# A fused attention and mixer kernel: a pair's keys loaded whole and first, and an order made with other times to landing

## The chip, the cores and the metric

The kernel runs on one core of one Trainium2 chip. The metric is the device time of one execution in microseconds (us). A core has five engines with a queue of instructions each: TensorE (PE; its weight loads are listed as PEld), VectorE (DVE), ScalarE (ACT), GpSimd (POOL) and SyncE (SP), which here issues every DMA.

## The reference

Three blocks follow one another, all in float32, with batch 4, 448 tokens and 768 channels:

- Attention, 12 heads of 64: `q` and `k` are divided by their root mean square along the head and multiplied by `g_q` and `g_k`; `scores = q_n k_n^T / 8`; softmax over the keys; times `v`.
- A gated mixer: `h = relu(x w_in)` (1024 wide), halves `u` and `v`; `v` is normalised, mixed over the tokens by `w_spatial` (448 x 448) plus a bias; `(u * v_s) w_out`.
- A second mixer: over the tokens (448 to 256 to 448) with a residual, then over the channels (768 to 1536 to 768) with a residual.

The softmax sums over all keys of a head, so the keys may stand in any order as long as the values stand in the same one.

## The kernel before, in words

Attention handles two heads at a time, a pair; there are 24 pairs (four batches of six). `Attention.load` (L593) fetches a pair's `q` and `k` into one tile `raw` of 112 partitions: 448 tokens are 4 chunks of 112, both heads side by side. There are two `raw` buffers. The 448 keys of a head are also cut as three chunks of 128 and a rest of 64 for the product with `v`; the rests of both heads are put together into one chunk of 128. For that the rest of the first head must stand at the end of its row of scores and the rest of the second at its beginning. In the kernel before the second head's keys are therefore loaded rotated, in three DMAs: the last 64 tokens first (64 rows), then the first 48 to fill the chunk, then the other 336. With two DMAs for `q` and one for the first head's `k` a pair takes six. `load_v` (L610) fetches `v` in four DMAs: for each head three chunks of 128, and the 64 of the rest into `vrest`.

`norms` (L622) squares and sums a pair on ACT and DVE (`sq`, `ss`; the half with `q` first, then the half with `k`; there is one `sq` buffer) and makes the factors `ra`, `ry`, `rz` on POOL and ACT; `scale` multiplies `raw` on POOL; `transposed` turns `q` and then `k` on PE into `tp` and copies it out (`whole` for the first eight pairs, `qt` and `kt` after them). `scores` (`sc`, `nm`, `e`), `normalise`, `turned` (`tp`, `et`) and `values` (`av`) follow. `start` (L751) does the first pair and loads the second; `slot` (L773) interleaves pair s with its neighbours and loads pair s + 2.

Beside attention run three kinds of work: conversions of weights on ACT, DVE and POOL (`word`, `wv`, `wpart`), of which the pieces of `prepare_uo` and `prepare_next` go through two buffers each of `wraw` and `wpart` and are stored to scratch in DRAM (`wu_d`, `wo_d` and others); and the first mixer, batch by batch (`vps`, `ups`, `sps`, `xps` on PE), which reads these weights back as `wu` and `wo`. After them come the token mixer (`h1ps`, `u_ps`) and the channel mixer (`h2ps`, `o_ps`).

The order in which every engine issues is not that of the source. All instructions are recorded in a `Plan`, each with a cost from `estimate` (L214): the time that it holds its engine and the lateness with which its result reaches the next engine. `issue` (L364) then places them by list scheduling on these costs: forward by priority, backward for new priorities, eight rounds, and the order of the shortest plan is issued, so that all instructions have the line L405 in the profile. For a DMA the costs are

```
        return max(475, shape[0] * n * 4 / 260), 2000
```

that is, SP is taken to be busy for 475 ns or for the bytes at 260 bytes a ns, and the data usable 2000 ns later. Every engine, SP too, issues strictly in the planned order.

Of the kernel before, what the change touches and what calls it, by code (L numbers as in the profile page):

```python
# [149 lines left out]
class Plan:  # L150
# [63 lines left out]
    def estimate(self, engine, fn, out, ins, kwargs):  # L214

        shape = max((tuple(x.shape) for x in [out] + ins if isinstance(x, Part)), key=free)
        n = free(shape)
        psum = any(x.tile.psum for x in ins)
        if engine == "tensor":
            if fn == "transpose":  # L220
                return ins[0].shape[0] / 1.2 + 3, 200
            n = free(ins[1].shape)
            if ins[1].dtype == F32R:
                return 0.326 * n if ins[0].shape[0] <= 64 else n / 2.4 + 13, 200
            if ins[0].shape[0] <= 64:
                return 1.04 * n, 200
            return n / 1.2 + 54 if out.shape[0] <= 64 else n / 0.6, 200
        if engine == "scalar":
            extra = any(isinstance(kwargs.get(k), Part) for k in ("bias", "scale"))
            extra += kwargs.get("accum_out") is not None  # L230
            return 0.833 * n + (51 if psum else 94) + 93 * extra, 142
        if engine == "vector":
            if n <= 64:
                return 160, 128
            if fn in ("tensor_scalar", "tensor_copy") and not psum:
                return 0.53 * n + 90, 128
            pointer = fn == "scalar_tensor_tensor" and any(free(x.shape) == 1 for x in ins)
            return 1.042 * n + 70 + 61 * pointer, 175 if free(out.shape) < n else 128
        if engine == "gpsimd":
            if fn == "tensor_scalar":  # L240
                return max(165, 1.3 * n + 35), 75
            pace = 2.0 if any(x.steps and x.steps[-1][0] == "to_broadcast" for x in ins) else 2.4
            return max(165, pace * n + 20), 75
        return max(475, shape[0] * n * 4 / 260), 2000

    def fence(self, pools, act):

# [173 lines left out]
def free(shape):  # L421
    n = 1
    for x in shape[1:]:
        n *= x
    return n
# [11 lines left out]
def attention_moe_mixer(  # L437
# [7 lines left out]
    nc = tc.nc  # L445
# [6 lines left out]
    P = 128  # L452
    C = 4
    T = S // C
# [10 lines left out]
    LAST, R = TOK[-1]  # L465
# [74 lines left out]
    nc = Plan(nc)  # L540
# [42 lines left out]
    class Attention:  # L583
# [9 lines left out]
        def load(self, i):  # L593
            if not 0 <= i < NP:
                return
            b, j = divmod(i, KD)
            t = self.p.tile([T, 2, C, 2, D], F32, tag="raw", bufs=2, name="raw")
            for r in range(2):
                nc.sync.dma_start(
                    out=t[:, 0, :, r], in_=q[b, 2 * j + r].rearrange("(c p) d -> p c d", p=T))  # L600
            nc.sync.dma_start(out=t[:, 1, :, 0], in_=k[b, 2 * j].rearrange("(c p) d -> p c d", p=T))

            src = k[b, 2 * j + 1]
            nc.sync.dma_start(out=t[:R, 1, 0, 1], in_=src[LAST:])
            nc.sync.dma_start(out=t[R:, 1, 0, 1], in_=src[:T - R])
            nc.sync.dma_start(
                out=t[:, 1, 1:, 1], in_=src[T - R:LAST].rearrange("(c p) d -> p c d", p=T))
            self.raw[i] = t

        def load_v(self, i):  # L610
            if not 0 <= i < NP:
                return
            b, j = divmod(i, KD)
            t = self.p.tile([P, 2, C - 1, D], F32, tag="v32", bufs=VB, name="v32")
            rest = self.rests[i % VB]
            for r in range(2):
                src = v[b, 2 * j + r]
                nc.sync.dma_start(out=t[:, r], in_=src[:LAST].rearrange("(c p) d -> p c d", p=P))
                nc.sync.dma_start(out=rest[r * R:(r + 1) * R, r], in_=src[LAST:])
            self.v32[i] = t, rest  # L620

        def norms(self, i):  # L622
# [597 lines left out]
    n = NP + 1  # L1220
# [84 lines left out]
```

## Time and profile before

| | |
|---|---|
| median of 3 runs | 956.19 us (954.49 to 959.67) |
| the profiled execution | 952.84 us, its span 951.1 us |
| PE busy | 915.1 us, 96% of the span |
| DVE busy | 567.9 us, 60% |
| ACT busy | 452.1 us, 48% |
| POOL busy | 370.1 us, 39% |
| DMA | 118.58 MB |

The span is the time from the first to the last recorded instruction; the execution's own time is 1.74 us longer. Matmuls are pipelined and their ends are modelled, so what counts of PE is where it has nothing to do rather than its busy share.

### The profile page before, as it was taken

To read this page: it belongs to the slowest core of one execution; us is meant where nothing else is said; L and a number is where in the kernel's file an instruction comes from. 1 tells how busy PE (TensorE), PEld (TensorE's weight loads), DVE (VectorE), ACT (ScalarE), POOL (GpSimd) and SP (SyncE) were. 2 spreads that over 40 slices of the span, in tenths; PEclk is the share of its full clock that TensorE was granted. 3 is DMA by queue.
4 is the path that set the end of the run, shared out by engine and by line. 5 is a ranking of instruction groups with operands and counts; after the bars stand their busy time and mean duration, and the time that the engine had idled before them with its cause. 6 is when DMAs were issued, how large, how long until landed. Compare 5 with 4: busy or idle time off the path is not lost.

```text
span 951.1 us, 15484 instructions
## 1 busy us (share of the span) xinstructions
PE 915.1 (96%) x5328; PEld 736.9 (77%) x5328; DVE 567.9 (60%) x1254; ACT 452.1 (48%) x1135; POOL 370.1 (39%) x538
## 2 busy tenths in 40 slices
PE   3898999999999999999999999999999999999998
PEld 1344366668767777677889999899898998999898
DVE  4787878775776767764151367534665556555434
ACT  5887877777676777765342345301312213122100
POOL 3767766785666664654124123101201102011100
PEclk9998999999999999999999999999999999999999
DMA  6544465666534565332673475721211212111024
GB/s 153 138 101 134 116 172 149 158 188 184 163 92 107 172 207 179 97 98 99 220 223 129 142 246 181 266 85 34 78 56 36 64 34 83 50 51 50 17 89 144
DMA packets 124654, 118.58 MB, mean 125 GB/s; under 512 B 74784, under 2 KB 108128, under 8 KB 123040
## 3 DMA queue, kind: packets, MB, share of 16 engines
q1 hardware_dynamic: 124576, 117.59, 41.0%
q8 instruction: 42, 0.69, 0.3%
q14 instruction: 36, 0.29, 0.1%
HBM read 89.77 MB, written 27.79 MB: 124 GB/s over the span
## 4 chain that ended last, share of the span: by engine, by line
PE 82%; ACT 5%; DVE 5%; DMA 3%; issue 2%; POOL 2%; SPq 1%; ACTq 0%; POOLq 0%; DVEq 0%
PE o_ps L405 18%; PE h2ps L405 18%; PE tp L405 9%; PE av L405 6%; PE xps L405 6%; PE ups L405 6%; PE sc L405 6%; PE sps L405 4%; PE u_ps L405 3%; PE h1ps L405 3%; PE vps L405 3%; ACT e L405 2%; DVE nm L405 1%; SPq L405 1%; DMA x<-x_d 1%
## 5 line engine op out<-in xcount | busy, mean ns | idle before, releaser
L405 PE MATMUL o_ps<-c,h 128*128 128x384 f32 x1008 | 179.7, 337 | 0.0
L405 PE MATMUL h2ps<-ut,c 128*128 128x512 f32 (+1 forms) x864 | 178.9, 364 | 0.0
L405 PEld LDWEIGHTS o_ps<-c,h 128*128 128x128 f32 x1008 | 175.0, 188 | 2.0 <-DVE acc L405 0.5
L405 PEld LDWEIGHTS h2ps<-ut,c 128*128 128x128 f32 x864 | 148.1, 189 | 24.3
L405 POOL TENSOR_SCALAR e<-e,sums 112x448 f32<-112x448 f32 x192 | 122.8, 656 | 63.0 <-DVE sums L405 35.1
L405 POOL TENSOR_TENSOR c<-word,c 128x384 fp32r<-128x384 f32 x40 | 40.5, 1014 | 265.1 <-ACT c L405 241.7
L405 ACT ACTIVATE e<-sc,nm 112x448 f32<-112x448 f32 x192 | 120.0, 637 | 29.1 <-PE tp L405 15.0
L405 DVE TENSOR_REDUCE nm<-sc 112x1 f32<-112x448 f32 x192 | 110.0, 614 | 22.3 <-PE sc L405 22.0
L405 PEld LDWEIGHTS tp<-ident,e 112*128 112x128 f32 x672 | 75.3, 142 | 47.0 <-POOL e L405 16.6
L405 PE MATMUL tp<-ident,e 112*128 112x112 f32 x672 | 101.9, 267 | 6.4 <-POOL e L405 3.2
L405 DVE TENSOR_TENSOR acc<-o_ps,acc 128x384 f32<-128x384 f32 x140 | 77.2, 555 | 29.6 <-PE o_ps L405 28.9
L405 ACT ACTIVATE h<-h2ps 128x512 fp32r<-128x512 f32 (+1 forms) x48 | 25.8, 538 | 116.5 <-PE h2ps L405 114.9
L405 ACT ACTIVATE c<-word 128x384 fp32r<-128x384 f32 x40 | 21.0, 525 | 123.0 <-DVE word L405 58.2
L405 DVE SCALAR_TENSOR_TENSOR h<-h2ps,h 128x512 fp32r<-128x512 f32 (+1 forms) x48 | 29.9, 624 | 82.3 <-ACT h L405 82.2
L405 ACT ACTIVATE et<-tp 128x448 f32<-128x448 f32 x120 | 63.4, 544 | 20.5 <-PE tp L405 19.9
L405 PE MATMUL ups<-xp,wu 128*128 128x448 f32 x288 | 69.6, 379 | 1.4 <-ACT vr L405 0.7
L405 PE MATMUL av<-et,v 128*64 128x448 f32 x288 | 67.4, 563 | 0.0
L405 PE MATMUL xps<-wo,g 128*128 128x256 f32 x432 | 63.3, 291 | 0.1
L405 PEld LDWEIGHTS xps<-wo,g 128*128 128x128 f32 x432 | 55.1, 190 | 5.0 <-issue 2.3
L405 PEld LDWEIGHTS ups<-xp,wu 128*128 128x128 f32 x288 | 51.7, 189 | 8.6 <-ACT vr L405 1.1
L405 DVE TENSOR_SCALAR word<-word 128x384 f32<-128x384 f32 (+1 forms) x92 | 34.2, 372 | 37.1 <-ACT word L405 35.7
L405 PE MATMUL vps<-wv,xp 128*128 128x512 f32 x216 | 55.1, 402 | 0.0
(105 smaller groups left out, 1414.5 us busy)
## 6 DMA issues: line engine op xcount, KB each, us to landing
raw<-in_moe_w_ch_dram SPq DMA_DIRECT2D x40, 384.0 KB, 3.2
wu<-wu_d SPq DMA_DIRECT2D x16, 768.0 KB, 5.1
wo<-wo_d SPq DMA_DIRECT2D x12, 1024.0 KB, 5.1
raw<-in_q_dram SPq DMA_DIRECT2D x48, 112.0 KB, 3.0
acc<-u_d SPq DMA_DIRECT2D x14, 384.0 KB, 8.2
out_dram<-o SPq DMA_DIRECT2D x28, 192.0 KB, 1.9
v<-in_v_dram SPq DMA_DIRECT2D x48, 96.0 KB, 2.6
x_d<-xo SPq DMA_DIRECT2D x36, 128.0 KB, 2.4
```

Of the source, the lines that this page charges most:

```text
L405: getattr(getattr(self.nc, op.engine), fn)(*args, **kwargs)
```

## The change

`load` fetches `k` of both heads in their natural order with one DMA each, and before `q`. A pair takes four DMAs instead of six. So that the rests still meet in one chunk, the second head's rest of keys is its first 64 tokens, and `load_v` fetches its values to match: the three chunks of 128 from token 64 on and the rest from the first 64. The lateness of a DMA in `estimate` becomes 2400 ns plus 1.2 ns for every 1000 bytes. What SP itself is taken to cost is the same formula as before. The whole order is planned anew on these numbers.

```diff
-        return max(475, shape[0] * n * 4 / 260), 2000
+        size = shape[0] * n * 4
+        return max(475, size / 260), 2400 + 1.2e-3 * size
...
-            for r in range(2):
-                nc.sync.dma_start(
-                    out=t[:, 0, :, r], in_=q[b, 2 * j + r].rearrange("(c p) d -> p c d", p=T))
-            nc.sync.dma_start(out=t[:, 1, :, 0], in_=k[b, 2 * j].rearrange("(c p) d -> p c d", p=T))
-
-            src = k[b, 2 * j + 1]
-            nc.sync.dma_start(out=t[:R, 1, 0, 1], in_=src[LAST:])
-            nc.sync.dma_start(out=t[R:, 1, 0, 1], in_=src[:T - R])
-            nc.sync.dma_start(
-                out=t[:, 1, 1:, 1], in_=src[T - R:LAST].rearrange("(c p) d -> p c d", p=T))
+            for a, src in ((1, k), (0, q)):
+                for r in range(2):
+                    nc.sync.dma_start(
+                        out=t[:, a, :, r], in_=src[b, 2 * j + r].rearrange("(c p) d -> p c d", p=T))
             self.raw[i] = t
...
                 src = v[b, 2 * j + r]
-                nc.sync.dma_start(out=t[:, r], in_=src[:LAST].rearrange("(c p) d -> p c d", p=P))
-                nc.sync.dma_start(out=rest[r * R:(r + 1) * R, r], in_=src[LAST:])
+                tiles, others = (src[R:], src[:R]) if r else (src[:LAST], src[LAST:])
+                nc.sync.dma_start(out=t[:, r], in_=tiles.rearrange("(c p) d -> p c d", p=P))
+                nc.sync.dma_start(out=rest[r * R:(r + 1) * R, r], in_=others)
```

## Rows read from the trace of the kernel before

**Rows 1.** Stretches: start:end, length, each engine's busy us (instructions), granted clock, DMA.

```profile
0.00:20.00 20.00, 5.29 (x18) 2.72 (x20) 6.44 (x13) 8.48 (x17) 6.99 (x20) 1.00 0.64 159
20.00:120.00 100.00, 86.81 (x469) 40.08 (x470) 81.86 (x180) 84.44 (x232) 73.86 (x118) 0.97 0.46 123
120.00:180.00 60.00, 57.03 (x336) 37.26 (x335) 49.16 (x138) 45.35 (x127) 39.32 (x62) 1.00 0.58 162
180.00:460.00 280.00, 279.17 (x1803) 204.87 (x1802) 181.90 (x433) 192.61 (x521) 171.42 (x268) 1.00 0.49 146
```

**Rows 2.** Waits of PE over the whole span: us in total, times, longest.

```profile
PE tp L405 <- POOL raw L405: 12.9, 1, 12.9
PE sc L405 <- ACT e L405: 4.9, 6, 1.5
...
PE sc L405 <- ACT whole L405: 3.2, 2, 1.8
```

**Rows 3.** Timeline of SP, first 14 us: start, length, instruction, count.

```profile
0.74 0.92 SPq L405 DMA_DIRECT2D raw<-in_q_dram  x2
1.71 2.18 SPq L405 DMA_DIRECT2D raw<-in_k_dram  x4
3.93 0.48 SPq L405 DMA_DIRECT2D g<-in_g_q_dram  x1
...
5.73 0.59 SPq L405 DMA_DIRECT2D g<-in_g_k_dram  x1
...
7.53 2.13 SPq L405 DMA_DIRECT2D raw<-in_k_dram  x4
9.71 0.47 SPq L405 DMA_DIRECT2D raw<-in_moe_w_in_dram  x1
```

**Rows 4.** Timeline of the other engines at the start; in brackets idle time and releaser.

```profile
3.78 0.63 ACT L405 ACTIVATE sq<-raw 112x512 f32<-112x512 f32 x1 [1.76 <-DMA raw<-in_q_dram]
...
5.62 0.63 ACT L405 ACTIVATE sq<-raw 112x512 f32<-112x512 f32 x1 [1.22 <-DMA raw<-in_k_dram]
...
8.11 0.16 DVE L405 TENSOR_TENSOR gg<-g 128x1 f32<-128x1 f32 x1 [2.99 <-DMA g<-in_g_k_dram]
8.19 0.68 DVE L405 TENSOR_REDUCE ss<-sq 112x8 f32<-112x512 f32 x1
...
8.96 0.20 POOL L405 TENSOR_SCALAR ra<-ss 112x16 f32<-112x16 f32 x1 [7.37 <-DVE gg L405]
...
12.89 1.76 PE L405 MATMUL tp<-ident,raw 112*128 112x112 f32 x8 [12.89 <-POOL raw L405]
...
14.79 0.66 ACT L405 ACTIVATE word<-raw 128x512 f32<-128x512 f32 x1 [2.74 <-DMA raw<-in_moe_w_in_dram]
15.36 0.53 ACT L405 ACTIVATE whole<-tp 128x448 f32<-128x448 f32 x1
15.78 0.63 ACT L405 ACTIVATE whole<-tp,gg 128x448 f32<-128x448 f32 x1
...
16.46 4.71 PE L405 MATMUL sc<-whole 64*112 64x448 f32 x12 [1.81 <-ACT whole L405]
```

**Rows 5.** Waits of ACT on DMAs between 20 and 180 us.

```profile
ACT wpart L405 <- DMA wo_d<-wpart: 1.3, 1, 1.3
ACT wpart L405 <- DMA wu_d<-wpart: 0.9, 3, 0.4
```

**Rows 6.** Pieces of SP's queue in the chain of waits, 120 to 180 us.

```profile
132.20 0.34 SPq L405
...
173.20 0.45 SPq L405
```

**Rows 7.** The page's DMA issues: count, KB each, median us to landing.

```profile
raw<-in_q_dram SPq DMA_DIRECT2D x48, 112.0 KB, 3.0
```

**Rows 8.** Two stretches in which the granted clock fell.

```profile
70.00:76.00 6.00, 5.12 (x23) 3.27 (x24) 3.39 (x7) 4.04 (x10) 5.50 (x12) 0.72 0.31 97
84.00:90.00 6.00, 4.61 (x16) 1.60 (x16) 4.89 (x10) 4.21 (x14) 5.73 (x11) 0.72 0.50 178
```

**Rows 9.** Instructions of `ups`: ns min/median/max, first and last start.

```profile
L405 PE MATMUL ups<-xp,wu x288: 358/368/475, 157.5 to 511.9; 128*128 128x448 f32 x144
```

## The prediction

> **What bounds the kernel now.** I read the busy time by stage first. PE is the bound nearly everywhere: from 180 to 460 us it is idle for 0.83 of 280 us, so nothing that only makes a load earlier can gain there. It has room in three stretches [rows 1]: 14.7 us of the first 20, 13.2 of the 100 after them, 3.0 of the 60 up to 180. In the second of these no engine is full (PE 87, ACT 84, DVE 82 us of 100): work hands over from engine to engine there, and the order decides. Then PE's list of waits: one wait of 12.9 us for the first scaled `raw`, and 3.2 us for `whole` in two waits [rows 2]; most of both lies in the first 17 us. So I read that start instruction by instruction.
>
> There SP is what sets the pace. It issues without a pause from 0.74 us on, some 0.54 us an issue (four take 2.18) [rows 3]. Behind the sixteen issues of two pairs and the four small `g` the first load of `w_in` is issued at 9.71 and usable at 14.79. ACT stands still 2.74 us for it, because `word` is ahead of `whole` in ACT's order; the `tp` that `whole` reads began at 12.89. Both copies then end at 16.41 and the first scores start at 16.46 [rows 4].
>
> **The change part by part.** *Two issues fewer a pair, at the start.* Four issues fewer stand before `w_in`: 4 x 0.54 = 2.2 us, so it is issued at 7.55 and, with the same 5.08 us to use, `word` runs at 12.6 to 13.3. The chain of norms has to be as early, and there `k` first works against it: the first `sq` reads `q`, which now is issued last. The fourth issue starts at 0.74 + 0.46 + 0.51 + 0.54 = 2.25; before, `q` was usable 2.58 after its second issue began (1.20 to 3.78), so `sq` of `q` runs 4.83 to 5.46, about a microsecond later than now, its sum (0.68) to 6.2, `sq` of `k` to 6.85, since there is one buffer, and its sum to 7.6. The `g` loads are issued 1.08 earlier, so `gg` moves from 8.11 to 7.03; if the second sum stays behind it, it ends at 7.9. `ra` comes at 7.6 to 7.9 instead of 8.96, PE's `tp` at 11.5 to 11.9 and ends by 13.6 [rows 3, 4]. The second `whole` can start at 13.7 behind `word` and the first `whole`, and the scores at 14.4 instead of 16.46: 2.0 us. Bounds: 2.2, all that the issues take, and 0, if something else that the plan puts ahead on ACT takes the place. I take 2.0, the value nearest to the rows.
>
> What the Trainium skill's page "DMA: Bandwidth & Descriptors" (section "Issuing engines are not separate DMA queues") says speaks against this: the time that a sequencer takes to initiate a DMA is usually small relative to the DMA. By that rule fewer issues would be worth nothing, 956.2 us, the first rival below. At the start of this trace it does not hold: 8.9 us of issues stand in front of a load that lands in 5.08.
>
> *Does the gain reach the end?* After 180 us PE has no idle time to swallow it. Between 20 and 180 it could be swallowed by a later chain that starts on its own; `load`, `norms` and conversions all hang on the same start, so I keep it whole; the other end, 0, is the first rival.
>
> *Two issues fewer in the other 22 pairs.* 44 x 0.54 = 24 us of SP. SP mostly waits there and is not the bound: the only waits of ACT on DMAs from 20 to 180 are 2.2 us, for buffers that stores hold, none for `raw` [rows 5]. In the chain of waits SP's queue has seven pieces longer than 0.05 us from 120 to 180, 2.7 us together [rows 6]. The bounds are 0 and 2.7; the value taken is 0.5, as a raw load's issues are a part of these only. After 180 nothing.
>
> *`k` before `q`, the other 64 tokens as the rest.* The bytes, the four DMAs for `v` and all the arithmetic stay. The loads run a pair ahead and ACT never waits for `raw` after the start, so the order within a load is hidden by that lead: 0; if the lead is gone, the microsecond worked out above for each pair.
>
> *The new times to landing.* They are costs of the plan, not work. For 112 KB the plan's landing goes from 475 + 2000 to 475 + 2538 ns; the trace has 3.0 us [rows 7], so the new number is right there. What a better number can give back directly is a wait for a load that was believed too early, and those are the 2.2 us just named, and the start. What remains is that the whole order is drawn anew. The trace bounds this only roughly: at best the 16.2 us of idle from 20 to 180 go, and with them the two falls of the granted clock to half, 1.2 GHz, each after PE had waited for other engines; they cost 2 x 6 x 0.28 = 3.4 us [rows 1, 8]. At worst PE starves longer: 6 us, the slower rival. Nothing in the rows leans to a side; I take 0.
>
> **Sum.** 952.84 - 2.0 - 0.5 = 950.3 us against the profiled execution (span 951.1 and 1.74 around it). The three runs have their median at 956.19, 3.35 above that execution, and their lowest above it too; on their scale the forecast is 953.7 us, and 952 to 955.5 is its own range.
>
> **The rivals.**
> - *The start's gain is lost*, behind another instruction on ACT or in the mixed stretch up to 120 us, or because `q` as the last load holds the norms: 956.2. For it: the work of ACT and DVE there is 84 and 82% and does not shrink. Against: PE must do the same work and starts earlier.
> - *The new order closes gaps.* If a third of the 16.2 us of idle and of the 3.4 us of clock goes, 6.5 us, on top of the start: 956.2 - 2.0 - 6.5 = 947.7; 944 to 951. For it: no engine is full in that stretch, and these gaps are hand-overs that an order can hide. Against: almost none of them is a wait for a DMA, the one cost that was corrected.
> - *The new order starves PE: slower.* A weight piece of 256 KB holds one of two buffers for a load and then a store of 128 KB each way. In the new plan the load is later by 715 ns and the store by 557: 1.27 us a round, and 12 rounds of two for the 24 pieces of `wu` and `wo` make 15 us. If the plan gives way there, the first `ups`, now at 157.5 [rows 9], comes at about 173, and PE has nothing to fill its gaps with. Then the idle share of 20 to 120, 13.2%, lasts from 120 to 173 or to 205: 7.0 or 11.2 us in place of 3.0 [rows 1], less the 2.0 of the start: 958.2 to 962.4. It decides from a first `ups` after 165. For it: the 13% stretch ends just when the first mixer's matmuls begin. Against: the pieces are not urgent in slots, and priority can pull them ahead.
>
> **Chances.** The forecast 0.38, the lost start 0.16, closed gaps 0.26, starved PE 0.20. The range from 946.5 to 960.5 leaves out the far thirds of the last two, some 0.07 and 0.10. A change under 0.5%, 4.8 us, can't be told from none with runs 5 us apart. Faster than that (below 951.4): nearly all of the closed gaps and a tail of the forecast, 0.30. Slower (above 961.0): about half of the starved case, a tail of the lost start, and the part of the plan's risk that I can't name, 0.15. Within: 0.55.
>
> **What would show it.** Right: `word` first at about 12.6 and the first `sc` at about 14.4; PE's idle time in the first 20 us down from 14.7 to about 12.7; 16 +- 3 us of idle from 20 to 180; under 1.5 us from 180 to 460; still no wait for `raw` after the start. A first `sc` after 15.5 refutes the start's step. A first `ups` after 165 with more idle before it is the slower rival; idle from 20 to 180 below 12 us, or a clock without the two falls, is the faster one. If PE's idle sum is unchanged but its busy time is not, all four cases are wrong, since each counts idle time alone.

## The result: 962.63 us, slower by 0.56%, and the profile after

Eight runs of the changed kernel have their median at 962.63 us (959.42 to 964.16), eight of the kernel before at 957.09 (953.28 to 959.67). The ratio is 1.0056, with a 95% interval from 1.0032 to 1.0081: 5.4 us slower, and outside the range. The profiled execution of after took 964.16 us (span 962.4), the slowest of its eight, and that of before (952.84) was faster than any of the other eight, so the 11.3 us between the two spans show about twice what the runs do. They are read here for where the time goes, and the ratios for how much.

The stretches of the kernel after, with the columns of [rows 1]:

```profile
0.00:20.00 20.00, 5.09 (x16) 2.49 (x16) 7.04 (x14) 8.51 (x18) 8.43 (x21) 1.00 0.77 177
20.00:120.00 100.00, 83.48 (x424) 40.38 (x425) 71.84 (x165) 76.38 (x208) 67.21 (x107) 0.91 0.43 119
120.00:180.00 60.00, 56.57 (x322) 34.78 (x321) 48.39 (x124) 44.16 (x122) 40.93 (x63) 1.00 0.50 145
180.00:460.00 280.00, 276.75 (x1765) 198.76 (x1764) 190.98 (x456) 197.96 (x538) 171.13 (x270) 1.00 0.49 143
```

PE is idle for 38.1 us of these 460, before for 31.7: 6.4 more, half of it from 20 to 120 us. In that stretch the granted clock fell from 0.97 to 0.91 in the mean. Three falls to 1.2 GHz are in these windows (the clock is the column after the five engines):

```profile
30.00:40.00 10.00, 8.16 (x36) 4.29 (x36) 5.65 (x12) 6.40 (x18) 8.53 (x17) 0.66 0.33 103
78.00:88.00 10.00, 7.04 (x30) 4.13 (x32) 5.12 (x14) 4.01 (x10) 6.88 (x13) 0.66 0.12 39
112.00:118.00 6.00, 4.44 (x27) 3.92 (x26) 3.65 (x8) 4.02 (x12) 5.45 (x10) 0.72 0.39 132
```

They take 10 x 0.34 + 10 x 0.34 + 6 x 0.28 = 8.5 us of full clock, against 3.4 before [rows 8]: 5.1 more. With the 6.4 of idle this is 11.5 of the 11.3. Over the whole span the same 5328 matmuls keep PE busy for 920.6 us instead of 915.1, and it is idle 5.8 us longer. In the typical run the clock counts for less: its recorded mean is 0.991 in the eight runs of after and 0.993 in the runs of before timed beside the experiments, an estimated 2 us of the 5.4. PE's waits over the whole span, as [rows 2], show what the idle time is:

```profile
PE tp L406 <- POOL raw L406: 12.0, 1, 12.0
PE tp L406 <- POOL e L406: 6.4, 11, 2.7
PE sc L406 <- ACT e L406: 5.9, 10, 1.5
...
PE sc L406 <- ACT whole L406: 2.5, 1, 2.5
```

and before, beside the second of these:

```profile
PE tp L405 <- POOL e L405: 3.2, 9, 0.7
```

The first wait is 0.9 shorter; what grew are hand-overs between engines. Then the start, SP first (as [rows 3]), then ACT and PE (as [rows 4]):

```profile
0.73 0.92 SPq L406 DMA_DIRECT2D raw<-in_k_dram  x2
1.70 1.02 SPq L406 DMA_DIRECT2D raw<-in_q_dram  x2
...
7.52 0.96 SPq L406 DMA_DIRECT2D raw<-in_moe_w_in_dram  x2
```

```profile
5.01 0.63 ACT L406 ACTIVATE sq<-raw 112x512 f32<-112x512 f32 x1 [3.00 <-DMA raw<-in_q_dram]
...
14.30 0.66 ACT L406 ACTIVATE word<-raw 128x512 f32<-128x512 f32 x1 [1.93 <-DMA raw<-in_moe_w_in_dram]
14.86 0.20 ACT L406 ACTIVATE ry<-ra 112x16 f32<-112x16 f32 x1
15.10 0.21 ACT L406 ACTIVATE ry<-ry 112x16 f32<-112x16 f32 x1
15.22 0.53 ACT L406 ACTIVATE whole<-tp 128x448 f32<-128x448 f32 x1
15.64 0.63 ACT L406 ACTIVATE whole<-tp,gg 128x448 f32<-128x448 f32 x1
```

```profile
12.03 1.76 PE L406 MATMUL tp<-ident,raw 112*128 112x112 f32 x8 [12.03 <-POOL raw L406]
16.32 3.33 PE L406 MATMUL sc<-whole 64*112 64x448 f32 x8 [2.54 <-ACT whole L406]
20.25 3.33 PE L406 MATMUL sc<-whole 64*112 64x448 f32 x8 [0.59 <-ACT e L406]
23.51 1.75 PE L406 MATMUL tp<-ident,raw 112*128 112x112 f32 x8
...
27.25 1.76 PE L406 MATMUL sc<-whole 64*112 64x448 f32 x8
```

`w_in` is issued at 7.52, as worked out (7.55), but usable only at 14.3 instead of 12.6, and ACT has two `ry` ahead of `whole`. The scores start at 16.32 instead of 14.4. From there the loss grows early: the 65th matmul of `sc` starts at 69.9 us instead of 63.6, the 129th at 142.1 instead of 132.0, and the end comes 11.3 later.

### The profile page after: what moved, and what is told of

Read it like the earlier page. It is cut to its first block, busy times and chain, and to the rows that moved or that the text cites. A ratio compares the mean times of both kernels' runs of the same rounds, so it can differ in the third digit from the quotient of the medians.

```text
span 962.4 us, 15406 instructions
## 1 busy us (share of the span) xinstructions
PE 920.6 (96%) x5328; PEld 738.4 (77%) x5328; DVE 570.1 (59%) x1254; ACT 453.0 (47%) x1135; POOL 371.5 (39%) x538
## 4 chain that ended last, share of the span: by engine, by line
PE 80%; ACT 7%; DMA 4%; POOL 3%; DVE 2%; issue 2%; SPq 1%; POOLq 0%; ACTq 0%
PE o_ps L406 18%; PE h2ps L406 17%; PE tp L406 8%; PE xps L406 6%; PE av L406 6%; PE ups L406 5%; PE sc L406 5%; PE vps L406 4%; PE sps L406 4%; PE u_ps L406 3%; PE h1ps L406 3%; ACT e L406 3%; SPq L406 1%; POOL e L406 1%; DMA raw<-in_q_dram 1%
## 5 line engine op out<-in xcount | busy, mean ns | idle before, releaser
L406 PE MATMUL tp<-ident,e 112*128 112x112 f32 x672 | 105.4, 271 | 9.6 <-POOL e L406 6.4
L406 ACT ACTIVATE c<-word 128x384 fp32r<-128x384 f32 x40 | 21.0, 525 | 128.3 <-DVE word L406 63.6
L406 PE MATMUL xps<-wo,g 128*128 128x256 f32 x432 | 60.8, 289 | 0.2 <-ACT e L406 0.2
L406 POOL TENSOR_TENSOR wpart<-wpart 128x256 fp32r<-128x256 f32 (+2 forms) x44 | 33.1, 752 | 62.5 <-ACT wpart L406 38.7
```

What stands on the lines that cost most here:

```text
L406: getattr(getattr(self.nc, op.engine), fn)(*args, **kwargs)
```

## The experiments

All are timed over five rounds against the kernel before on the same chip. Theory A: the loss comes from the new lateness itself. Theory B: from `k` first and `q` last. Theory C: from drawing the order anew, whatever the numbers are. Two came up on the way. Theory D: `k` first costs time only where a plan leaves the first square no lead over the landing of `q`. Theory E: a part of the loss is the half clock at which PE starts.

**One part alone, planned anew.** `e1` has the new lateness and the six loads; `e2` the four loads, `k` first, and the old lateness.

```diff
 # e1: the kernel before with
-        return max(475, shape[0] * n * 4 / 260), 2000
+        size = shape[0] * n * 4
+        return max(475, size / 260), 2400 + 1.2e-3 * size
 # e2: the kernel after with this undone
```

> The six loads of before, with the new lateness of a DMA; everything planned anew. Theory A (the loss of 5.5 us comes from the lateness, through the order it makes): 960 to 965 us, the ratio to before 1.003 to 1.009. Theory B (the loss comes from k first and q last, which holds the norms): 955 to 959, ratio within 0.002 of 1. Theory C (any new plan of this kernel lands several us to either side, whatever the edit): anything from 0.990 to 1.012, not tied to the other runs.

> The four loads of after, k first, with the old lateness; planned anew. Theory A: the same as before or up to 2.5 us faster, 954 to 957, as the two issues fewer were predicted to save 2 at the start. Theory B: 960 to 965, like after. Theory C: anything from 0.990 to 1.012.

Measured: `e1` 1.0021 (1.0004 to 1.0039), `e2` 1.0034 (1.0013 to 1.0056). Each part alone is slower, and neither carries the loss alone. `e1` fits neither A (from 1.003) nor B (within 0.002 of 1); `e2` is where B expected it, and C allows both.

**One part alone, in a fixed order.** `e3` plans with the six loads of before and its lateness, and then issues two whole loads for each of `q` and `k` in the places of the first four and nothing in the other two. On PE, ACT, DVE and POOL the instructions stand exactly as before. `e4` does the reverse: the order of after, but the second head's `k` in three issues, with the rotated keys, all three in the place of one.

```diff
 # e3, in load(), after the six loads are recorded
+            six = nc.ops[-6:]
+            calls = [whole loads of q, q, k, k]
+            for op, call in zip(six, calls + [None, None]):
+                op.call = call
```

> The order of before, instruction for instruction on every engine; only two of the six issues of each pair are left out (q first, then both k whole). It measures the saved issues by themselves. Theories A and C: 2.0 us faster by the working of the prediction (first scores at 14.4 instead of 16.5 us); 0 if the load of w_in lands no earlier, as in after, where it took 6.8 us instead of 5.1. Theory B, whose cost is k first: the same here.

> The order of after, instruction for instruction; only the second head's k is loaded in three issues again, with the rotated keys. It prices the order by itself. Theories A and C: 961 to 967 us, as slow as after or up to 3 us slower. Theory B: still slow too, as k is first; but if the order were innocent and the number of issues mattered, 955 to 958.

Measured: `e3` 0.9975 (0.9956 to 0.9994), 2.4 us faster than before (0.6 to 4.2); `e4` 1.0134 (1.0106 to 1.0163). So in the order of before the saved issues are worth what the prediction said, within that interval, and the loss is in the order and in what the order makes of the loads. `e4` missed its forecast: 961 to 967 us was expected, at most 3 us slower than after, and 970.62 came, 0.8% slower than after. The order of after thus loses far more by the two further issues than the order of before does. They stand ahead of `q`, and ACT's first squares wait longer for it, 3.4 us in all against 1.7 in after:

```profile
ACT sq L406 <- DMA raw<-in_q_dram: 3.4, 4, 1.1
```

So `e4` prices the order together with that wait, and not by itself. The start of `e3`, ACT and then PE:

```profile
13.35 0.66 ACT L407 ACTIVATE word<-raw 128x512 f32<-128x512 f32 x1 [2.77 <-DMA raw<-in_moe_w_in_dram]
```

```profile
11.91 1.75 PE L407 MATMUL tp<-ident,raw 112*128 112x112 f32 x8 [11.91 <-POOL raw L407]
15.03 4.88 PE L407 MATMUL sc<-whole 64*112 64x448 f32 x12 [1.36 <-ACT whole L407]
```

The scores start 1.43 us earlier than before [rows 4]. The forecast of 2.0 is missed by `w_in`, usable at 13.35 instead of 12.6. At the 65th matmul of `sc` 1.3 us of the gain are left (62.3 instead of 63.6), at the 129th nothing (132.8 instead of 132.0). With the fastest execution of before in that pair, the two profiles can't show whether the gain at the start reaches the end; that 2.4 us do is the ratio's word.

**`k` first or `q` first.** `e7` is after with `q` first: the planned order is the same on every other engine. `e10` is after, with `norms` squaring the half with `k` first. `e9` is `e3` with `k` first.

```diff
 # e7
-            for a, src in ((1, k), (0, q)):
+            for a, src in ((0, q), (1, k)):
 # e10
-            for h in (slice(0, n // 2), slice(n // 2, n)):
+            for h in (slice(n // 2, n), slice(0, n // 2)):
```

> The kernel after, with q before k as in the kernel before; its planned order is the same as after's on every other engine, so only the order of the four issues differs. Theory B (k first holds the norms): 2 to 5 us faster than after, ratio to before 1.000 to 1.004. Theories A and C: within 1.5 us of after, ratio 1.004 to 1.007; at the start the first sq comes about a microsecond earlier, but its second half waits for k.

> The kernel after with the same order, but norms squares the half with k first, so that what is loaded first is used first. Theories B and D (the wait of the first square for q, the last load, is the cost of k first): back to the level of the run with q first in this order, 1.000 to 1.004. If k first cost through something else (the transfers themselves): as after, 1.004 to 1.007.

> The order of before on every engine, the four loads with k first. Theory D (k first costs time only where a plan leaves the first square, which reads q, no lead over the landing; before's order has 1 to 4 us of lead in pairs 2 to 4): like the run with q first in this order, ratio 0.997 to 0.999, with only the start up to 1 us later. Theory B (k first costs 3.7 us in any order): 1.000 to 1.003.

Measured: `e7` 1.0017 (0.9999 to 1.0034), `e10` 1.0017 (0.9997 to 1.0036), `e9` 0.9997 (0.9974 to 1.0020). Against after's 1.0056, turning the loads round or turning the squares round gives back the same 0.4%. So it is not the order of the transfers that costs time, but that the first square waits for the last load. The squares of pairs 2 to 4 on ACT, `sq` of the first half of each, first in after, then in `e7`, then in `e10`:

```profile
21.74 0.63 ACT L406 ACTIVATE sq<-raw 112x512 f32<-112x512 f32 x1
...
29.67 0.63 ACT L406 ACTIVATE sq<-raw 112x512 f32<-112x512 f32 x1 [0.82 <-DMA raw<-in_q_dram]
...
45.87 0.63 ACT L406 ACTIVATE sq<-raw 112x512 f32<-112x512 f32 x1 [0.88 <-DMA raw<-in_q_dram]
```

```profile
21.09 0.62 ACT L406 ACTIVATE sq<-raw 112x512 f32<-112x512 f32 x1
...
28.39 0.63 ACT L406 ACTIVATE sq<-raw 112x512 f32<-112x512 f32 x1
...
42.66 0.65 ACT L406 ACTIVATE sq<-raw 112x512 f32<-112x512 f32 x1
```

```profile
20.64 0.62 ACT L406 ACTIVATE sq<-raw 112x512 f32<-112x512 f32 x1
...
27.81 0.61 ACT L406 ACTIVATE sq<-raw 112x512 f32<-112x512 f32 x1
...
41.24 0.65 ACT L406 ACTIVATE sq<-raw 112x512 f32<-112x512 f32 x1
```

In after ACT waits twice for `q`, the last load; in the others it does not. This wait, between 18 and 180 us, is 3.3, 2.1 and 3.2 us in three other plans with `k` first (`e2`, `e14` and `e13` below) and 1.1, 0 and 0 with `q` first in the same orders (`e11`, `e16` and `e15`).

In after the waits are only 1.7 us, but the delay against `e7` is 0.65, 1.3 and 3.2 us at the three squares, and then hardly grows: PE's `tp` of pair 4 starts at 63.91 in after and 60.73 in `e7`. How it grows from the second to the third, PE in after and then in `e7`, and a window of each with its clock:

```profile
30.96 1.01 PE L406 MATMUL sc<-whole 64*112 64x448 f32 x4 [1.52 <-ACT e L406]
...
35.53 1.76 PE L406 MATMUL av<-et,v 128*64 128x448 f32 x4 [0.88 <-ACT et L406]
37.22 1.01 PE L406 MATMUL tp<-ident,raw 112*128 112x112 f32 x4
```

```profile
35.01 0.97 PE L406 MATMUL av<-et,v 128*64 128x448 f32 x4 [0.97 <-ACT et L406]
35.91 0.60 PE L406 MATMUL tp<-ident,raw 112*128 112x112 f32 x4
```

```profile
32.00:39.00 7.00, 6.12 (x22) 2.92 (x23) 4.07 (x9) 3.76 (x11) 5.53 (x10) 0.52 0.26 86
32.00:39.00 7.00, 6.03 (x42) 3.41 (x40) 4.87 (x11) 4.70 (x12) 5.44 (x10) 1.00 0.22 75
```

In after `e` stands on ACT behind the square that was held, PE waits 1.52 us for it, and then the granted clock is at half, 1.2 GHz. So the transposes of pair 2 begin 1.3 us later than in `e7` and end 2.1 later. The loads of pair 4 wait for these transposes to free their `raw` buffer; they are issued at 40.01 instead of 37.90, and the next square waits for `q` once more. So about half of the 3.2 us is the half clock, which `e7` does not have there in its profile, and 0.5 was there at the first scores (16.32 and 15.83), as `w_in` landed later. That the fall of the clock belongs to `k` first is not shown by one pair of profiles; that the swap costs 0.4% is. ACT's waits for `q` over the whole span, in after and then in `e7`:

```profile
ACT sq L406 <- DMA raw<-in_q_dram: 14.1, 9, 3.0
ACT sq L406 <- DMA raw<-in_q_dram: 5.0, 3, 2.1
```

Five of after's nine, 7.9 us, come later than 180 us. PE is idle only 1.7 us longer than in `e7` between 180 and 460 us, and the delay of 3.2 us at pair 4 is 4.3 at the end.

In the order of before the same swap costs 0.2% by the medians of the ratios, with intervals that overlap, and ACT shows no wait for `q` between 18 and 180 us there; theory D expected less, B more. By the trace's landing events the first squares of pairs 2 to 4 start 4.2, 2.8 and 2.3 us after `q` has landed with `q` first (`e3`), and 2.9, 0.1 and 1.3 with `k` first.

**The size of the lateness.** `e5`, `e8` and `e6` are after with 2420, 2380, and 2538 without the term in the size.

```diff
-        return max(475, size / 260), 2400 + 1.2e-3 * size
+        return max(475, size / 260), 2420 + 1.2e-3 * size   # e5; e8: 2380
+        return max(475, size / 260), 2538                   # e6
```

> The kernel after, with 2420 ns in place of 2400 as the lateness of a DMA: 20 ns more for each, a change too small to be right or wrong about the chip, but it redraws the order (hundreds of lines on PE and ACT). Theory A (the size of the lateness is what makes the order bad): as after, ratio to before 1.003 to 1.008. Theory C (every new plan is a fresh draw, and the one of before was a good draw): it may land anywhere from 0.995 to 1.015, and several thousandths from after's 1.0056.

> The kernel after, with 2380 ns in place of 2400: the other neighbour of its plan. Theory A: as after, 1.003 to 1.008. Theory C: unrelated to after and to the run with 2420, 0.995 to 1.015.

> The kernel after, with 2538 ns of lateness for every DMA, the value of a 112 KB load, and no term in the size. Theory A in the form that large loads of weights, believed late, are put ahead of the pairs' loads: 955 to 958 us, ratio 0.996 to 1.001, since that preference is gone. Theory C: unrelated to after, 0.995 to 1.015.

Measured: 1.0059, 1.0070 and 1.0057. With after's 1.0056, four different orders agree within 0.14%. That spoke for A and against C, and flat 2538 as slow as the rest speaks against the term in the size. So the other side was tried: four loads with a flat lateness of 2000 and its neighbours, and 1600.

> Four loads, q first, the old lateness, planned anew; the same order on the other engines as the run with k first and the old lateness (1.0034). With these it completes the square of k or q first by old or new lateness. Theory A with B: 0.996 to 1.001, 0.2 to 0.4% below both the run with k first and the run with the new lateness and q first (1.0017). Theory C: no such sum, 0.995 to 1.010.

> As the run before, with the lateness taken too short, 1600 ns. Theory A (a load believed late has its consumers queued behind other work, so less is better): as fast or faster than with 2000 ns, 0.994 to 1.000. Theory C: unrelated to it, 0.995 to 1.010.

> Four loads, k first, 1980 ns of lateness: a neighbour of the plan with 2000 (1.0034). If the new lateness itself costs time, this stays near that run, 1.002 to 1.005, below the four plans around 2400 (1.0056 to 1.0070). If each plan is a draw, it is not tied to it, and 1.006 or more is as likely as less.

> The same with 2020 ns. If the new lateness itself costs time: 1.002 to 1.005. If each plan is a draw: untied, 0.999 to 1.010.

> Four loads, q first, 1980 ns; the order of the run with k first and 1980 ns. If k first costs what it did in the three pairs so far (0.2 to 0.4%), it is that much faster than it. If the lateness counts: 0.998 to 1.002.

> Four loads, q first, 2020 ns; the order of the run with k first and 2020 ns. Again 0.2 to 0.4% faster than it if k first costs time; 0.998 to 1.002 if the lateness counts, untied if each plan is a draw.

| lateness | k first | q first |
|---|---|---|
| 2400 + 1.2e-3 x size | 1.0056 (after) | 1.0017 (`e7`) |
| 2000 | 1.0034 (`e2`) | 1.0002 (`e11`) |
| 2020 | 1.0023 (`e14`) | 0.9990 (`e16`) |
| 1980 | 1.0094 (`e13`) | 1.0053 (`e15`) |
| 1600 | | 1.0104 (`e12`) |
| the order of before | 0.9997 (`e9`) | 0.9975 (`e3`) |

Each interval is 0.2 to 0.4% to either side. Read across: `q` first is faster in all five pairs, by 0.39, 0.32, 0.33, 0.41 and 0.22%; in each pair the other engines run one and the same order in both traces. Read down: 20 ns on the lateness, one per cent, moves the time by up to 0.6%, and 40 ns by up to 0.7%. The four plans around 2400 lie inside the spread of the three around 2000, so their agreement was no proof of A; C stands, and whether the new lateness costs anything beyond its draw these runs can't tell. `e12` falsifies A's other half, that less is better. The order of before is the best in both columns, though its interval overlaps that of `e16`: it was itself a good draw.

**The half clock at the start.** Between `e3` and `e7` (0.42%, 4.0 us; 4.8 in their spans) PE's idle time differs by only 1.3 us up to 460 us, and by 0.8 over the whole span. The other 4.0 are busy time: the same matmuls take 919.0 us instead of 915.0, and 3.3 of that are the scores of the first eight pairs. Their sums, in `e3` and then in `e7`, and the first four scores that run at full speed in each:

```profile
L407 PE MATMUL sc<-whole 64*112 64x448 f32 x128 | 32.6, 608 | 6.6 <-ACT e L407 3.5 <-ACT whole L407 2.9
L406 PE MATMUL sc<-whole 64*112 64x448 f32 x128 | 35.9, 663 | 5.8 <-ACT e L406 3.6 <-ACT whole L406 2.0
```

```profile
20.57 1.01 PE L407 MATMUL sc<-whole 64*112 64x448 f32 x4
32.68 1.01 PE L406 MATMUL sc<-whole 64*112 64x448 f32 x4
```

In `e7` three groups of eight scores up to 30 us take 3.33 us each, where they take 1.76 later; in `e3` twelve scores without a pause come first, and PE is at full speed 12 us earlier. Whether the kernel would end earlier without the half clock, the sums don't say: PE might only wait longer instead. To remove that, 72 transposes of the identity that nobody reads were put on PE ahead of the first pair.

```diff
+    warm = psum.pool.tile([P, 512], F32, tag="bank0", bufs=1, name="warm")
+    for _ in range(72):
+        nc.nc.tensor.transpose(warm[:, :P], ident, ident)
```

> The kernel after with 72 transposes of the identity put on PE ahead of all else, where it waits 12 us for the first pair; nothing reads what they write. Theory E (a part of the loss is the half clock at which PE works until some time after 25 us: eight scores take 3.33 us there and 1.76 later): the first eight scores in under 2.5 us, the second group in 1.8, and 2 to 4 us less than after, ratio to before 1.0015 to 1.0035. If the half clock at the start is hidden behind ACT and DVE: as after, 1.0045 to 1.007.

> The four loads with q first in the order of before (0.9975), with the same 72 transposes at the start. Theory E: 2 to 3 us less than without them, as twelve scores take 4.9 us there at the half clock and 2.6 at the full one: ratio 0.994 to 0.996, the fastest of all. If hidden: 0.9965 to 0.9985.

Measured: `e17` 1.0068 (1.0039 to 1.0098), `e18` 1.0010 (0.9987 to 1.0034): no gain, rather a loss. The start of `e17`, PE and then a window within the first eight scores with its clock:

```profile
1.36 9.65 PE L563 MATMUL warm<-ident 128*128 128x128 f32 x72 [1.36 <-POOL ident masks.py:199]
12.08 0.98 PE L406 MATMUL tp<-ident,raw 112*128 112x112 f32 x8 [1.07 <-POOL raw L406]
16.03 3.33 PE L406 MATMUL sc<-whole 64*112 64x448 f32 x8 [2.97 <-ACT whole L406]
```

```profile
16.00:19.00 3.00, 2.97 (x8) 1.07 (x8) 2.48 (x5) 1.61 (x3) 2.84 (x3) 0.50 1.28 235
```

The transposes did bring the full clock: the first `tp` takes 0.98 instead of 1.76. After the pause of 2.97 us before the scores it was gone again (0.50 while they ran) and the scores were as slow as without. The edit did not remove what it was to price, so theory E is neither shown nor refuted. The window does show that 3.33 us for eight scores is the time at 1.2 GHz.

## Why the prediction was wrong, by its own steps

**The issues left out: right.** The forecast was 2.0 us at the start and 0.5 after it. In the order of before they give 2.4 (`e3`, 0.6 to 4.2). That the sum agrees so well is in part luck: the start gave 1.43 in the trace, as the landing of `w_in` was mis-sized, 5.83 us from its issue in place of 5.08, and where the rest comes from is open. In after nothing of it reaches the scores (16.32 against 16.46): the load took 6.8 us, and two `ry` went ahead. What made it 6.8 is not shown; with the same issues behind it in the same order it took 6.3 in `e7` and 5.8 in `e10`. That is the rival of the lost start, as far as the start goes. The remark that issues are not small here set sixteen of them, 8.9 us, against one landing: one issue, 0.54 us, is small beside the 2.6 us in which the median `raw` load of the first 24 us lands, and it is their number that counts.

**`k` before `q`, priced at 0: wrong, and this step failed.** The prediction saw that the first `sq` reads what is loaded last, and that it costs a microsecond a pair if the lead is gone. It took the lead from the trace of before, where ACT never waits for `raw`, without counting it: the first squares of pairs 2 to 4 start 3.6, 2.6 and 1.0 us after `q` has landed there. And the lead belonged to that order. The plan made with the change left the first square 0.1 us or less in pairs 2 to 4. The cost is 0.39% or 3.7 us, shown twice at an unchanged order (`e7`, `e10`), and with the same sign in four more pairs with one order each. Over 22 pairs of heads that is far less than the microsecond a pair that was named: the later waits stand where PE mostly has other work.

**The new order, priced at 0: wrong too.** With the same four loads, `q` first, it costs 0.42% or 4.0 us against the order of before (`e7` against `e3`). That the rows leaned to neither side was right of them; what was overlooked is that the order in hand was the better end of a spread: six plans with four loads and `q` first span 0.9975 to 1.0104, and all five that were drawn anew (0.9990 to 1.0104) are slower than the one of before. Where these 4.0 us lie is not settled: in one pair of profiles most of the difference is time at the half clock, and that could not be taken out to price it.

The sum is -0.25% + 0.42% + 0.39% = +0.56%, the measured ratio. It closes by its making, as each term is the step from one kernel to the next: before, `e3`, `e7`, after.

**The rivals.** The starved PE is the one that comes nearest in time, and its mark was met: the first `ups` came at 165.5, past the 165 from which it was to decide. Its mechanism was not at work. By the 33rd matmul of `sc` 4.8 us were lost (43.4 against 38.6), before the first weight piece was stored (64.6), and the idle time from 120 to 180 us is 3.4, near the old 3.0, where it needed 7. The sentence that PE's idle time alone carries every case was also too narrow: 5.1 of the 11.3 us between the profiles went to the falls of its clock. Of the marks for being right none was met: the first `sc` came at 16.32, PE was idle for 14.9 us of the first 20, 19.95 from 20 to 180 and 3.25 from 180 to 460, and after the start ACT waited for `raw` seven times.

## What to carry to other kernels

An edit that makes a planner draw the whole order anew is two changes; issue the edit in the old order too, or its own worth can't be seen (here -2.4 us, inside a kernel 5.4 us slower). Before a new constant is believed, move it by one per cent: what that moves the time is the noise of the planner, here up to 0.6%. And load first what is used first: a swap of two loads is free only as long as the order keeps a lead, and that lead is a property of the order, not of the loads. The version that beats both kernels is `e3`, the four loads with `q` first in the order of before, at 0.9975 (0.9956 to 0.9994).

## What the runs showed of the hardware beyond that

- Loads that are issued sooner do not always land sooner. The first two loads of `v` were issued 1.7 us earlier in after than in before, behind two loads of `w_in` instead of one, and landed about a microsecond later; with the same issues in `e10` they took 6.4 to 6.6 us and landed when they do in before. The issue and the times to landing, least, median and most, in before and then in after:

```profile
L405 SPq DMA_DIRECT2D v<-in_v_dram x2: 427/456/486, 10.2 to 10.7; - x2
DMA to landing us min/median/max: 4.9/4.9/5.0
```

```profile
L406 SPq DMA_DIRECT2D v<-in_v_dram x2: 433/648/862, 8.5 to 9.0; - x2
DMA to landing us min/median/max: 7.7/7.7/7.7
```

- The record of the granted clock reads 1.00 before its first change, also where PE's durations show half of it: in after eight scores take 3.33 us at 16.32 and 20.25 and 1.76 at 27.25, in windows that read 1.00 (the first of the stretches of after above, and 16 to 24 and 27 to 29 us). The durations, not the record, tell the clock there.
